# Reading Z and Bs back in the pieces that one unit wrote

## The chip, the cores and the metric

The kernel runs on one core of a Trainium2 chip. The metric is the device time of one execution in microseconds (us). The engines are PE (TensorE, matmuls), PEld (its weight loads), DVE (VectorE), ACT (ScalarE), POOL (GpSimd) and SP (SyncE, which here only issues DMAs). DMAs that SP issues stand in the profile's queue q1, those of POOL in q0; 16 DMA engines move the data of both.

## The reference

The kernel computes a Fourier layer with a feed-forward block behind it, for 8 sequences of 3008 rows of 256 values:

```
X = rfft(x, axis=1)                                # x: (8, 3008, 256)
Yr = Xr @ w_r - Xi @ w_i + b_r
Yi = Xr @ w_i + Xi @ w_r + b_i
Yr, Yi = soft-threshold of each at 0.01            # sign(Y) * max(|Y| - 0.01, 0)
y = irfft(Yr + i Yi, n=3008)
h = y @ w_in                                       # 256 -> 2048
out = elu(h) @ w_out                               # 2048 -> 256, float32
```

## The kernel before

3008 is 47 x 64, and both transforms are done as two matmul stages with a transposition between them. One sequence is a batch b, and its spectral part is cut into units, each a few matmuls into PSUM and one evacuation to bf16:

- A (`unit_A`, L129): 6 units, 4 of 24 column groups j each. M1 (128 x 128) makes the 64-point transform. The result, 128 rows (4 blocks of 32: half, real or imaginary) for each j, is written to a DRAM tensor DA [24, 128, 256].
- The transposition: `load_Z` (L159) reads DA back so that the 96 partitions of Z are (j, block) and the 32 slots of a block lie along the partition: row p = 4j + block. It is cut by slots, so that each read takes from all that the six A units wrote. Batch 0 has four reads of 8 slots (384 KB each), the others one of 8 and one of 24 slots.
- X (`unit_X`, L166): 8 units, two for every 8 slots. Each matmul contracts over the 96 partitions of one slot of Z with a table M2, whose rows are in the same order as those of Z.
- M (`m_group` L185, `unit_M`, `first_M` L220): 12 units, product with w_r and w_i, bias, soft-threshold. In steady batches the bias is the float tensor bias_bc, added on DVE (L202). In batch 0 some units have it added by PE instead (L189): a matmul of ones with bias_p, which holds the bias as three bf16 pieces in three of its rows.
- B (`unit_B`, L233): 6 units with table M3, written to DRAM as DB [24, 128, 256]. `load_Bs` (L267) reads it back as Bs, cut by slots like Z: four reads of 8 slots, 384 KB each, into four buffers.
- Y (`unit_Y`, L274): 8 units with table M4, two for each Bs read. They make yT, the input of the feed-forward part.

The feed-forward part runs over blocks of 512 rows: `front` (L705) multiplies with w_in and takes exponentials, `finish_elu` and `elu` finish the activation, `back` (L757) multiplies with w_out and stores. A batch has 47 steps of it. `plan` (L800) puts the spectral units of the next batches (b+1: X, M, B, Y; b+2: A) into the steps of batch b, one or two per step; `f0` runs ahead of a step's `front`, `f1` behind it. The order on each engine is the order of the program.

Batch 0's spectral part has nothing to run beside; this opening is written out by hand (L505 to L679), and its order matters here:

1. POOL reads x of batch 0 in six pieces between the iotas that make the tables. DVE and ACT make M1, then the A units run as x lands, each followed by its write of DA on SP.
2. Meanwhile DVE and ACT make M2 (`points`, `phases`, `wraps`, `sizes`, `signs`, `sines`), whose phases start from columns that depend on the row p (half and block: `qcol`, `c0`, `c1`).
3. SP then reads w_r and w_i (L518), Z in four pieces (L164), bias_bc (L527), and the first quarter of w_in (L578), which must wait until the scratch pool of the tables is free. POOL casts w_r and w_i to bf16 (L520 to L523).
4. On POOL a `gate` (a tiny copy that reads a landed tile, L588) holds back the reads of x for batch 1 until the second Z read has landed; behind them follows the first half of w_out (L583).
5. X units; between them DVE makes the three bias pieces (L602 to L610). Then M3 (L613 to L621), M and B units, DB writes, quarters 1 and 2 of w_in, and after the last B the Bs reads (L271), the A units of batch 1, the scaling of w_in (L658), and the first two Y units.

`idle_pe` (L295) issues matmuls without use that keep PE going.

Of the kernel before, what the change touches and what calls it, by code (L numbers as in the profile page):

```python
# [29 lines left out]
def kernel(  # L30
# [47 lines left out]
    zp = ctx.enter_context(tc.tile_pool(name="zp", bufs=1))  # L78
    wk2 = ctx.enter_context(tc.tile_pool(name="wk2", bufs=2))
    wk3 = ctx.enter_context(tc.tile_pool(name="wk3", bufs=3))  # L80
    wk4 = ctx.enter_context(tc.tile_pool(name="wk4", bufs=4))
# [47 lines left out]
    def unit_A(b, u, alone=False, on_dve=False, ahead=False):  # L129
        ci, uu = u // 2, u % 2  # L130
        if uu == 0:
            if ahead and ci > 0:
                A_of[b, ci] = late3.tile([P, 8, D], BF16, name="A", tag="gT")
            elif alone:
                A_of[b, ci] = wk4.tile([P, 8, D], BF16, name="A", tag="Bs")
            else:
                A_of[b, ci] = wk2.tile([P, 8, D], BF16, name="A", tag="A")
            if ci == 0:
                DA_of[b] = dram.tile([NJ, P, D], BF16, name="DA", tag="DA")
        xt, A = xts[ci], A_of[b, ci]  # L140
        dav = DA_of[b].rearrange("j p d -> p j d")
# [9 lines left out]
        )  # L151
        j0 = 8 * ci
# [6 lines left out]
    def load_Z(b, s0, s1):  # L159

        if b not in Z_of:
            Z_of[b] = zp.tile([2 * NR, NS, D], BF16, name="Z", tag="Z")
        dv = DA_of[b].rearrange("j (h c s) d -> (j h c) s d", h=2, c=2)
        nc.sync.dma_start(Z_of[b][:, s0:s1, :], dv[:, s0:s1, :])  # L164
# [102 lines left out]
    def load_Bs(b, w):  # L267

        Bs = wk4.tile([4 * K1, 8, D], BF16, name="Bs", tag="Bs")
        dv = DB_of[b].rearrange("k (c h m) d -> (k c h) m d", c=2, h=2)  # L270
        nc.sync.dma_start(Bs[:], dv[:, 8 * w : 8 * w + 8, :])  # L271
        Bs_of[b, w] = Bs

    def unit_Y(b, u, alone=False, on_dve=False):  # L274
# [3 lines left out]
        yT, Bs = yT_of[b], Bs_of[b, w]  # L278
        ps = unit_ps("yps", alone)
        psv = ps[:].rearrange("p a (k j) -> p (a k) j", j=P)  # L280
        for j in range(8):
            nc.tensor.matmul(  # L282
                psv[:, j, 0 : 2 * N1], lhsT=Bs[:, j, dt * P : dt * P + P], rhs=M4[:],
# [16 lines left out]
    brow, rest = (wk3.tile([P, 2 * D], F32, name="yb", tag="yb") for _ in range(2))  # L300
    nc.vector.memset(brow[:], 0.0)
    for o, bv in ((0, b_r), (D, b_i)):
        for k in range(3):
            nc.sync.dma_start(
                brow[32 * k : 32 * k + 1, o : o + D],
                bass.AP(tensor=bv.tensor, offset=bv.offset, ap=[[0, 1], [1, D]]),
            )
    idle_pe(9)
    xts = []
# [3 lines left out]
    with tc.tile_pool(name="stagep", bufs=1) as stagep:  # L313
# [41 lines left out]
        pcol = iota("pcol", [P, 1], [[0, 1]], cm=1)  # L355
        srow = iota("srow", [P, 2 * NS], [[0, 2], [1, NS]])
# [52 lines left out]

        k4h = col(dve, qcol, 0.5, ALU.mult, -0.25, ALU.add)  # L410
# [87 lines left out]
        pool.tensor_tensor(v4[:], v4[:], r4[:], ALU.subtract)  # L498

# [17 lines left out]
        fA(5)  # L517
        nc.sync.dma_start(w_r_f[:], w_r.rearrange("(c p) e -> p c e", p=P))  # L518
        nc.sync.dma_start(w_i_f[:], w_i.rearrange("(c p) e -> p c e", p=P))
        pool.tensor_copy(wcat_r[:, :, 0:D], w_r_f[:])  # L520
        pool.tensor_copy(wcat_r[:, :, D : 2 * D], w_i_f[:])
        pool.tensor_scalar(wcat_s[:, :, 0:D], w_i_f[:], -1.0, None, ALU.mult)
        pool.tensor_copy(wcat_s[:, :, D : 2 * D], w_r_f[:])  # L523
        for g in range(4):
            load_Z(0, 8 * g, 8 * g + 8)
# [36 lines left out]
        idle_pe(40)  # L562
# [10 lines left out]
    def load_w_in(q):  # L573
        if q < 3:
# [10 lines left out]
    def gate(src):  # L585

        t = gatep.tile([P, 1], F32, name="gate", tag="gate")
        nc.gpsimd.tensor_copy(t[0 : src.shape[0], :], src)  # L588
# [6 lines left out]
    gate(Z_of[0][:, 8, 0:1])  # L595
    for ci in range(3):
        load_x(1, ci)
    load_w_out(0)
    nc.vector.tensor_scalar(w3[:], v3[:], CMAGIC, -CMAGIC, ALU.add, ALU.add)
    nc.vector.tensor_tensor(w3[:], v3[:], w3[:], ALU.subtract)  # L600
    nc.scalar.copy(bias_p[:], brow[:])
    nc.vector.tensor_tensor(rest[:], brow[:], bias_p[:], ALU.subtract)  # L602
    for u in range(8):
        unit_X(0, u, alone=True, on_dve=u in (1, 4, 7))
        if u == 1:
            nc.scalar.activation(a3[:], w3[:], AF.Abs)
            nc.vector.tensor_copy(bias_p[32:64], rest[32:64])
            nc.vector.tensor_copy(bias_p[64:P], rest[64:P])
            nc.vector.tensor_tensor(rest[64:P], rest[64:P], bias_p[64:P], ALU.subtract)
            nc.vector.tensor_copy(bias_p[64:P], rest[64:P])  # L610
        idle_pe(1)
# [14 lines left out]
    nc.scalar.activation(r4[:], v4[:], AF.Sin, bias=0.0, scale=TURN)  # L626
    nc.scalar.activation(dume[:], busy[:, 0:1], AF.Exp, scale=0.0)
# [3 lines left out]
    load_w_in(1)  # L631
    first_M(2, 1, True)
    first_M(3, 0, False)
    fB(1)
    first_M(3, 1, True)
    first_M(4, 0, False)
    fB(2)
    first_M(4, 1, True)
    first_M(5, 0, True)
    fB(3)  # L640
    load_w_in(2)
    first_M(5, 1, True)
    let_go()
    fB(4)
    idle_pe(3)
    fB(5, True)
    M4v = M4[:].rearrange("p (a h) -> p a h", h=2)
# [4 lines left out]
    load_Bs(0, 0)  # L652
    load_Bs(0, 1)
# [8 lines left out]
    scale_w_in(0, True)  # L662
    for u in range(6):
        unit_A(1, u, on_dve=bool(u % 2), ahead=True)
        if u == 1:
            scale_w_in(1, True)
            for w in (2, 3):
                load_Bs(0, w)
            gate(Bs_of[0, 2][:, 0, 0:1])
            load_w_out(1)  # L670
            load_w_in(3)
        idle_pe(2)
    scale_w_in(2, False)
    for s0, s1 in ((0, 8), (8, NS)):
        load_Z(1, s0, s1)
# [124 lines left out]
    def plan(b):  # L800
# [18 lines left out]
        for t, u in enumerate(seq, lead):  # L819
# [9 lines left out]
            if u == ("A", 1):  # L829
# [69 lines left out]
```

## Time and profile before

| | us |
|---|---|
| time, median of 3 runs (912.48 to 912.52) | 912.52 |
| the profiled execution's own time | 911.36 |
| its span, first to last instruction | 909.6 |
| first A matmul | 5.93 |
| first read of Z issued | 18.40 |
| first X matmul | 23.25 |
| first M matmul | 29.77 |
| last B's matmuls end | 46.82 |
| first Y matmul | 55.16 |
| first `front` matmul | 56.54 |
| first Y of batch 1 | 149.35 |
| mean granted clock of TensorE | 0.997 |

Busy shares are taken over the whole span, so they hide the opening, a sixteenth of it. To read the opening one goes by the chain in order of time, which follows the work that ended last back through what released it, and by the timeline and the windows of the first 60 us.

### The profile page before, as it was taken

How to read it: one execution, taken by the hardware profiler on the slowest of the kernel's cores; microseconds unless marked ns; L12 is line 12 of the kernel's file. 1: busy time of each engine (PE TensorE's matmuls, PEld its weight loads, DVE VectorE, ACT ScalarE, POOL GpSimd, SP SyncE). 2: the span in 40 equal slices, each digit the busy share in tenths (PEclk: the TensorE clock that was granted, in tenths of full speed). 3: DMA queues.
4: the chain of work that ended last, by engine and by line, in shares of the span. 5: the costliest groups of instructions: out<-in, count | busy, mean ns of one | idle time of the engine just before them, and what ended most of it. 6: DMA issues, size and time to landing. Idle time of an engine off the chain costs nothing.

```text
span 909.6 us, 17270 instructions
## 1 busy us (share of the span) xinstructions
PE 893.2 (98%) x6721; PEld 652.3 (72%) x6721; DVE 717.5 (79%) x891; ACT 696.8 (77%) x850; POOL 314.9 (35%) x438
## 2 busy tenths in 40 slices
PE   8989999999999999999999999999999999999997
PEld 3447667876688667886678766787667866777775
DVE  8669778887788778897788877888778877778776
ACT  6768788777878778787787888778887877767664
POOL 6701540333321441405404153033332134443664
PEclk9999999999999999999999999999999999999999
DMA  8997116721283215732166032752228111231011
GB/s 270 309 269 228 47 48 186 209 70 47 77 241 124 71 47 143 190 109 85 56 201 194 24 99 59 217 161 72 69 72 230 30 42 47 82 82 48 24 48 46
DMA packets 90670, 106.24 MB, mean 117 GB/s; under 512 B 5270, under 2 KB 81308, under 8 KB 87228
## 3 DMA queue, kind: packets, MB, share of 16 engines
q1 hardware_dynamic: 84332, 77.62, 30.6%
q0 software_dynamic: 5968, 27.26, 9.1%
q8 instruction: 52, 0.85, 0.4%
q10 hardware_dynamic: 288, 0.26, 0.1%
q14 instruction: 30, 0.25, 0.1%
HBM read 55.32 MB, written 49.81 MB: 116 GB/s over the span
## 4 chain that ended last, share of the span: by engine, by line
PE 85%; DVE 5%; ACT 3%; DMA 3%; issue 2%; POOL 1%; SPq 1%; DVEq 0%; ACTq 0%; POOLq 0%
PE ps_o L773 34%; PE hps L715 34%; PE mps L192 9%; PE yps L282 2%; PE bps L244 2%; PE xps L175 2%; PE aps L144 2%; DMA Bs<-DB 2%; DVE gT L742 1%; DVE Et L754 1%; ACT Et L729 1%; ACT Et L726 1%; DMA xt<-in_x_dram 1%; DVE osb L784 1%; ACT Bz L257 1%
## 5 line engine op out<-in xcount | busy, mean ns | idle before, releaser
L773 PE MATMUL ps_o<-w_out_r,gT 128*128 128x256 f32 x3008 | 477.0, 301 | 0.2 <-DVE gT L740 0.2
L773 PEld LDWEIGHTS ps_o<-w_out_r,gT 128*128 128x128 f32 x3008 | 403.4, 189 | 50.3 <-DVE osb L784 1.3
L715 PE MATMUL hps<-yT,w_in_s 128*128 128x512 bf16 (+4 forms) x1728 | 389.9, 353 | 2.5 <-DVE gT L742 1.2
L740 DVE SCALAR_TENSOR_TENSOR gT<-Et,hps 128x512 fp32r<-128x512 f32 (+1 forms) x272 | 222.8, 848 | 75.3 <-POOL Et L752 38.2
L742 DVE SCALAR_TENSOR_TENSOR gT<-hps,Et 128x1024 fp32r<-128x1024 f32 x198 | 242.2, 1223 | 16.5 <-PE ps_o L773 1.0
L715 PEld LDWEIGHTS <-w_in_s 128*128 128x128 bf16 x1728 | 141.6, 98 | 129.4 <-issue 23.0
L729 ACT ACTIVATE Et<-hps 128x1024 f32<-128x1024 f32 x198 | 204.0, 1030 | 13.2 <-PE hps L715 6.7
L752 POOL TENSOR_SCALAR Et<-Et 128x512 f32<-128x512 f32 x187 | 111.4, 615 | 222.9 <-ACT Et L724 222.9
L754 DVE TENSOR_SCALAR Et<-Et 128x1024 f32<-128x1024 f32 x198 | 137.0, 692 | 48.0 <-ACT Et L729 40.1
L210 POOL TENSOR_SCALAR clip<-yb 128x512 f32<-128x512 f32 x84 | 51.7, 615 | 316.0 <-DVE yb L202 278.6
L724 ACT ACTIVATE Et<-hps 128x512 f32<-128x512 f32 x188 | 102.1, 595 | 63.9 <-PE hps L715 63.9
L726 ACT ACTIVATE Et<-hps 128x1024 f32<-128x1024 f32 x84 | 86.3, 1027 | 71.5 <-PE hps L715 71.0
L211 POOL TENSOR_TENSOR Y<-yb,clip 128x512 bf16<-128x512 f32 x84 | 107.2, 1276 | 7.0
L727 ACT ACTIVATE Et<-Et 128x1024 f32<-128x1024 f32 x84 | 88.8, 1058 | 2.7
L202 DVE TENSOR_TENSOR yb<-mps,bias_bc 128x512 f32<-128x512 f32 x89 | 61.4, 689 | 35.4 <-PE mps L192 28.6
L127 ACT CAST XT<-xps 128x768 bf16<-128x768 f32 x61 | 48.8, 800 | 15.8 <-PE xps L175 15.8
L127 ACT CAST yT<-yps 128x752 bf16<-128x752 f32 x63 | 49.7, 788 | 14.2 <-PE yps L282 14.1
L192 PE MATMUL mps<-wcat_r,XT 128*128 128x512 bf16 x192 | 58.2, 384 | 0.8 <-ACT Bz L257 0.3
L127 ACT CAST A<-aps 128x1024 bf16<-128x1024 f32 x45 | 45.6, 1014 | 15.3 <-PE aps L144 13.8
L192 PE MATMUL mps<-wcat_s,XT 128*128 128x512 bf16 x192 | 57.1, 379 | 0.0
L192 PEld LDWEIGHTS <-XT 128*128 128x128 bf16 x384 | 30.8, 98 | 29.6 <-DVE XT L125 0.6
L257 ACT CAST Bz<-bps 128x1024 bf16<-128x1024 f32 x46 | 46.0, 1000 | 2.5 <-PE bps L244 2.5
(110 smaller groups left out, 412.9 us busy)
## 6 DMA issues: line engine op xcount, KB each, us to landing
xt<-in_x_dram POOLq DMA_DIRECT2D x21, 1024.0 KB, 7.1
out_dram<-osb SPq DMA_DIRECT2D x158, 128.0 KB
Bs<-DB SPq DMA_DIRECT2D x32, 384.0 KB
DA<-A SPq DMA_DIRECT2D x21, 512.0 KB
DB<-Bz SPq DMA_DIRECT2D x21, 512.0 KB
Z<-DA SPq DMA_DIRECT2D x7, 1152.0 KB
Z<-DA SPq DMA_DIRECT2D x11, 384.0 KB
xt<-in_x_dram POOLq DMA_DIRECT2D x6, 512.0 KB, 5.9
```

Of the source, the lines that this page charges most:

```text
L127: nc.scalar.copy(dst, src)
L192: nc.tensor.matmul(ps, lhsT=XT[:, dt, c, o : o + P], rhs=wm[:, dt, :], start=(not biased and m == 0 and dt == 0), stop=(m == 1 and dt == 1),)
L211: nc.gpsimd.tensor_tensor(Y_of[b, q][:, i, :], yb, clip[:], ALU.subtract)
L715: nc.tensor.matmul(hps[:, s, c0:c1], lhsT=w_in_s[:, dt, ft * P : ft * P + P], rhs=yT_of[b][:, dt, t0 : t0 + c1 - c0], start=(dt == 0), sto ...
L724: nc.scalar.activation(E_[:, s], hps[:, s], AF.Exp)
L726: nc.scalar.activation(E_, hps[:], AF.Relu, scale=-1.0)
L729: nc.scalar.activation(E_, hps[:], AF.Exp)
L740: nc.vector.scalar_tensor_tensor(o, e, -1.0, h, ALU.add, ALU.max)
L742: nc.vector.scalar_tensor_tensor(o, h, 0.0, e, ALU.max, ALU.add)
L752: eng.tensor_scalar(E_[:, s], E_[:, s], 1.0, 0.0, ALU.min, ALU.max)
L754: nc.vector.tensor_scalar(E_, E_, 1.0, -1.0, ALU.min, ALU.add)
L773: nc.tensor.matmul(po[q][:, i_ % 2, :], lhsT=gT[:, s, i_ * P : i_ * P + P], rhs=w_out_r[:, ft, :], start=(ft == 0 and i_ % 2 == 0), stop=( ...
```

## The change

- **Reads of Z and Bs.** A read now takes what one unit wrote: the four j (or k) of unit u, 256 KB that lie together in DRAM, as 16 rows of 16 KB. They go to every sixth partition of Z, u, u + 6, ..., u + 90. There are six reads per batch for Z and six for Bs. Bs becomes one tile of all 32 slots in a pool with one buffer (batch 0's A shares it).
- **Tables.** The row p of Z and Bs now stands for i + 16u, where p = 6i + u. Seven more operations on DVE (`sixth` to `c0`) and one iota on POOL (`p16`) make this number as `zcol` and from it `qcol`, `c0`, `c1`, from which M2 and M4 follow as before.
- **Bias pieces.** The bias is read as 128 partitions of four values, split into three pieces by five small POOL operations, written to DRAM (`bd`) and read back into three rows of bias_p. The 128 x 512 arithmetic on DVE and ACT goes.
- **Opening requests.** SP: after the A writes come `bd`, Z reads 0 to 3, bias_p, Z reads 4 and 5, then w_r, w_i and bias_bc. The casts of w_r and w_i move from POOL to DVE, between X units. The wrap of M3's phase (`w3`) moves from DVE to POOL. The gate of batch 1's x now looks at w_i. Each Bs read of batch 0 follows one write of DB later on; w_in's quarter 1 stands behind the second of them, quarter 2 behind all six, quarter 3 behind A of batch 1. The absolute value for M3 moves behind the X units, the sine for M4 ahead of them, and the load of the Exp table behind the last B.
- **Steady batches.** Two Z reads follow each second A unit a step later, two Bs reads each second B unit (not ahead of the last Y unit of the batch before). w_in's quarters 2 and 3 are scaled by DVE in halves behind steps 1 to 4.

The diff, cut to its core:

```diff
-    def load_Z(b, s0, s1):
+    def load_Z(b, u):
 
         if b not in Z_of:
             Z_of[b] = zp.tile([2 * NR, NS, D], BF16, name="Z", tag="Z")
-        dv = DA_of[b].rearrange("j (h c s) d -> (j h c) s d", h=2, c=2)
-        nc.sync.dma_start(Z_of[b][:, s0:s1, :], dv[:, s0:s1, :])
+        dv = DA_of[b][4 * u : 4 * u + 4].rearrange("j (r s) d -> (j r) s d", r=4)
+        nc.sync.dma_start(Z_of[b][u : 2 * NR : 6], dv)
...
-    def load_Bs(b, w):
+    def load_Bs(b, v):
 
-        Bs = wk4.tile([4 * K1, 8, D], BF16, name="Bs", tag="Bs")
-        dv = DB_of[b].rearrange("k (c h m) d -> (k c h) m d", c=2, h=2)
-        nc.sync.dma_start(Bs[:], dv[:, 8 * w : 8 * w + 8, :])
-        Bs_of[b, w] = Bs
+        if b not in Bs_of:
+            Bs_of[b] = bsp.tile([P, NS, D], BF16, name="Bs", tag="Bs")
+        dv = DB_of[b][4 * v : 4 * v + 4].rearrange("k (r m) d -> (k r) m d", r=4)
+        nc.sync.dma_start(Bs_of[b][v : 4 * K1 : 6], dv)
...
-    brow, rest = (wk3.tile([P, 2 * D], F32, name="yb", tag="yb") for _ in range(2))
-    nc.vector.memset(brow[:], 0.0)
...
+    for o, bv in ((0, b_r), (P // 2, b_i)):
+        nc.sync.dma_start(b4[o : o + P // 2, :], bv.rearrange("(p j) -> p j", j=4))
+    bd = dram.tile([P, 3, 4], BF16, name="bd", tag="bd")
+    nc.vector.memset(bias_p[:], 0.0)
...
         pcol = iota("pcol", [P, 1], [[0, 1]], cm=1)
+        p16 = iota("p16", [P, 1], [[0, 1]], cm=16)
...
+        sixth = col(dve, pcol, 1.0 / 6.0, ALU.mult, -5.0 / 12.0, ALU.add)
+        rcol = col(dve, sixth, CMAGIC, ALU.add, -CMAGIC, ALU.add)
+        zcol = mix(dve, rcol, -95.0, p16, ALU.mult, ALU.add)
+        half = col(dve, zcol, 0.5, ALU.mult, -0.25, ALU.add)
+        qcol = col(dve, half, CMAGIC, ALU.add, -CMAGIC, ALU.add)
+        c1 = mix(dve, qcol, -2.0, zcol, ALU.mult, ALU.add)
+        c0 = col(dve, c1, -1.0, ALU.mult, 1.0, ALU.add)
...
+        for k in range(3):
+            pool.tensor_copy(bp3[:, k, :], b4[:])
+            if k < 2:
+                pool.tensor_tensor(b4[:], b4[:], bp3[:, k, :], ALU.subtract)
...
         fA(5)
+        nc.sync.dma_start(bd[:], bp3[:])
+        for u in range(6):
+            load_Z(0, u)
+            if u == 3:
+                nc.sync.dma_start(
+                    bias_p[0:3, :].rearrange("k (p j) -> k p j", j=4),
+                    bd.rearrange("p k j -> k p j"),
+                )
         nc.sync.dma_start(w_r_f[:], w_r.rearrange("(c p) e -> p c e", p=P))
         nc.sync.dma_start(w_i_f[:], w_i.rearrange("(c p) e -> p c e", p=P))
-        pool.tensor_copy(wcat_r[:, :, 0:D], w_r_f[:])
...
-        for g in range(4):
-            load_Z(0, 8 * g, 8 * g + 8)
...
+        nc.scalar.activation(r4[:], v4[:], AF.Sin, bias=0.0, scale=TURN)
+        pool.tensor_scalar(w3[:], v3[:], CMAGIC, -CMAGIC, ALU.add, ALU.add)
+        pool.tensor_tensor(w3[:], v3[:], w3[:], ALU.subtract)
+        idle_pe(37)
...
+        for u in range(8):
+            unit_X(0, u, alone=True, on_dve=u in (1, 4, 7))
+            if u in (1, 4):
+                for dst, src, sc in casts[u // 2 : u // 2 + 2]:
+                    dve.tensor_scalar(dst, src[:], sc, None, ALU.mult)
+            if u == 0:
+                t = stagep.tile([P, 1], F32, name="gate")
+                pool.tensor_copy(t[:], w_i_f[:, 1, D - 1 : D])
+                for ci in range(3):
+                    load_x(1, ci)
+            idle_pe(1)
...
     load_w_in(0)
-    gate(Z_of[0][:, 8, 0:1])
-    for ci in range(3):
-        load_x(1, ci)
     load_w_out(0)
...
+    nc.scalar.activation(a3[:], w3[:], AF.Abs)
...
     fB(1)
+    load_Bs(0, 0)
...
     fB(2)
+    load_Bs(0, 1)
+    load_w_in(1)
...
     fB(3)
-    load_w_in(2)
+    load_Bs(0, 2)
...
     fB(4)
+    load_Bs(0, 3)
     idle_pe(3)
     fB(5, True)
+    load_Bs(0, 4)
+    load_Bs(0, 5)
+    load_w_in(2)
+    nc.scalar.activation(dume[:], busy[:, 0:1], AF.Exp, scale=0.0)
...
     scale_w_in(0, True)
+    gate(Bs_of[0], 64, 4 * K1, 0)
+    load_w_out(1)
     for u in range(6):
         unit_A(1, u, on_dve=bool(u % 2), ahead=True)
+        if u % 2:
+            write_A(1, u)
...
-            if u == ("A", 1):
-                f1[t] += [(load_Bs, (n1, w)) for w in range(4)]
-            if u == ("A", 5) and n2 < B:
-                f1[t] += [(load_Z, (n2, s0, s1)) for s0, s1 in ((0, 8), (8, NS))]
+            if u[0] == "B" and u[1] % 2:
+                at_ = max(t, seq.index(("y", 7)) + lead) + 1
+                f1[at_] += [(load_Bs, (n1, u[1] - 1)), (load_Bs, (n1, u[1]))]
+            if u[0] == "A" and u[1] % 2 and n2 < B:
+                f1[t + (u[1] < 5)] += [(load_Z, (n2, u[1] - 1)), (load_Z, (n2, u[1]))]
```

## The prediction

> **What bounds the kernel now.** I read the page first, then the chain of work in order of time, then the opening's timeline, windows and DMA answers. The page says that this is a TensorE kernel:
>
> ```profile
> span 909.6 us, 17270 instructions
> PE 893.2 (98%) x6721; PEld 652.3 (72%) x6721; DVE 717.5 (79%) x891; ACT 696.8 (77%) x850; POOL 314.9 (35%) x438
> ```
>
> After about 57 us the chain is nearly all matmuls, and a read that is early there is worth nothing. The chain in order of time shows where transfers set the end (start, length, what):
>
> ```profile
> 6.12 7.21 DMA xt<-in_x_dram
> ...
> 29.48 0.97 DVE XT L125
> ...
> 30.50 0.82 PE mps L192 x3
> ...
> 48.19 2.77 DMA DB<-A
> ...
> 51.15 3.97 DMA Bs<-DB
> ...
> 55.16 0.85 PE yps L282 x16
> ```
>
> The reader is to see one round trip of DB on the path: write 2.77, read 3.97. The round trip of DA is not in the chain but in the timeline:
>
> ```profile
> 18.40 1.74 SPq L164 DMA_DIRECT2D Z<-DA  x4
> ...
> 23.25 0.51 PE L175 MATMUL xps<-M,Z 96*128 96x96 bf16 x8 [0.43 <-DMA Z<-DA]
> ```
>
> The four reads of Z are issued from 18.40, when all of DA is written, and the first X starts at 23.25 with only the first of them landed; the seventh X waited for the fourth read, until 27.63. In the steady part PE's waits show Bs late twice, at 149.35 and 797.83:
>
> ```profile
> PE yps L282 <- DMA Bs<-DB: 1.9, 2, 1.0
> ```
>
> The DMA engines themselves are full for most of the opening (columns end with clock, DMA share, GB/s), and while POOL's queue has a transfer going, a younger one of SP's does not move: DB's first write is issued at 36.82, and the DMA answer for 37 to 39 us lists it among the issues but has packets of q0 (POOL's) alone:
>
> ```profile
> 36.00:38.00 2.00, 2.00 (x15) 0.85 (x15) 0.64 (x2) 0.80 (x1) 1.83 (x3) 1.00 1.22 379
> ...
> q0 software_dynamic: 685, 0.75, 161.6%
> ...
> DB<-Bz SPq DMA_DIRECT2D x1, 256.0 KB
> ```
>
> The packet records say the same for DA's first write (issued 7.85, first packet about 11.4, when the reads of x end).
>
> **The change, step by step**, for batch 0 (times before -> after).
>
> *Ahead of Z.* One more iota stands ahead of the reads of x on POOL: 0.14 (row of pcol): all reads of x, and DA's last write, +0.14. Seven one-column operations on DVE (0.15 to 0.17 each, 1.1 in all) delay the tables; DVE idles 0.73 at 12.73 and the tables end near 21.5, ahead of the first X: nothing, as long as X does not start before 21.6. The three bias pieces are five small POOL operations (0.19 to 0.58) after 13.84: done by 14.9 to 16.9, beside DA's last packets, which end at 17.3: nothing.
>
> *Z.* SP has the six reads behind DA's writes; the first four need only writes that landed long before, so their packets follow DA's at 17.3 where they began at 19.2 (w_r and w_i, 0.5 MB, went first): -1.9. Against it, every X contracts over all 96 partitions, so the first X now needs all six reads, not one of four. The same 1.5 MB goes to the same rows, now as 16 rows of 16 KB a read, one for each of 16 DMA engines. By the packet records a 4 KB packet took 0.245 us, a 12 KB one of Z 0.80: 16 KB is 1.0 to 1.07, six of them 6.0 to 6.4, as 24 of 4 KB were (5.9). I take the old landing of the last read: 27.63 - 1.9 + 0.14 = 25.9. The read of bias_p stands ahead of the last two reads: 384 packets of 8 bytes. The nearest rows are 9 ns (4 bytes) and 27 ns (512 bytes): spread over 16 engines 0.2 to 0.65, on fewer engines more (rival 4); I take 0.3. First X: 23.25 -> 26.2, **+2.95**.
>
> *X.* Eight units; ACT has five evacuations of 0.80, DVE three of 0.95, and PSUM two buffers. The 3.15 us of bias arithmetic leave DVE, four casts of weights (0.42, row of w_in_s 128x512) come in, each pair right after an evacuation and done before DVE's next one. Stepping the two buffers through gives 6.5 from first X to last evacuation; before it was 7.2. First M: 30.50 -> 32.7, **+2.2**. The casts need w_i at 28.3: its packets end about 26.8 (25.3 + 32 packets of 46 ns an engine); just covered.
>
> *M and B.* The absolute value for M3 (0.85) stood between X units on ACT; now it and two sines (0.85, 0.92) follow the last X, and DVE's product for M3 (0.96) stands ahead of the first M's bias add on DVE, which comes 1.1 later after the first M. Three PSUM buffers absorb part: PE loses between 0 and 0.9, I take 0.6. PE is full from there (2.00 of 2.00 in the windows). Last B ends 46.83 -> 49.6, **+2.8**. The wrap of M3's phase on POOL (0.92 + 1.91 from its 128x512 rows) ends near 24.7: hidden. The Exp table load (1.28 + 0.20) moves behind the last B, ahead of the first A of batch 1 on ACT.
>
> *Bs.* The reads of x for batch 1 now wait for w_i (27.6, gate 0.4, issue 28.1, was 26.19): with w_out's first half they hold the engines until 41.4 (was 39.5). SP's first quarter of w_in waits for the casts (about 31 instead of 25.6): it is younger than these, so it goes after 41.4, and so do DB's writes. Behind 41.4 stand two quarters of w_in (1.3 each), six writes (0.8), six reads of Bs (1.0), and SP waits in order: each read for its write's landing (packets' end + 0.9), with the next write queued behind it. Stepped through, DB's last write lands at 54.8 (was 50.97) and the last read at 57.7: 54.9 + 0.9 to the first packet + 1.0 + 0.9. Y could not start before 57.5 anyway (last B + 7.9: table load, six units of A in two PSUM buffers, then a buffer). First Y: 55.15 -> 57.8, **+2.65**.
>
> *Later.* Batch 1's Z: last read lands about 74 and X comes at 75.4: nothing, at most 2. From batch 1 on, four of six Bs reads and of six Z reads come long before need: a gain off the path. The two places where Bs is late now need the last two reads (512 KB, 2.0) instead of the first of four (384 KB, six packets of 0.245: 1.5): +0.5 each, **+1.0**; if something else than the size held them, these waits could vanish (-2.2). w_in's scaling in DVE's halves (0.42) is covered in slots that PE bounds.
>
> Sum: 2.65 + 1.0 = **+3.65 us**. Against the profiled execution (span 909.6, time 911.36) that is 915.0; the median of the runs, 912.52, lies 1.16 above it, so I predict 916.2.
>
> **Rivals.**
> 1. *Read rate* (faster). Reads with one 16 KB run an engine could go at the rate of x's rows (8 KB in 0.325): 0.65 instead of 1.0 each. Then all of Z lands at 17.3 + 3.9 + 0.9 + 0.44 = 22.5, the first M comes 1.5 earlier, and the first Y is set by A at 45.9 + 7.9 = 53.8: -1.35; late waits -0.3; without the 0.6 in M -2.25: 910.3 to 910.9, say 910.5. It decides where a Z packet of 16 KB takes under about 0.8. For it: the first Z packets of 4 KB took 0.18. Against: 12 KB packets took 0.80, and instruction fetches of 16 KB 1.05.
> 2. *It washes out.* If Z's stragglers come from the bias reads mixed in behind them (last packet near 26.8, the mass done by 25.3), Z lands at 24, the first M and the last B stay where they are, Y starts with A's end at 54.7 to 55.3, and the late waits add up to 1.0: +0 to +1.1, say 913.1.
> The Trainium skill (SBUF — State Buffer, Door 1: The DMA port swizzle) puts 64 of these 96 partitions on one half of the ports. Its 435 GB/s over 16 ports would make their 1 MB over eight ports an estimate of 4.8 us, where the packet rows make 6.0 for Z; by the page Z would land at 23.4, the first Y come at 54.7, and the time be about 912.3.
> 3. *The reads go one by one.* It doesn't do what it says, if every sixth partition counts as an overlap with the read before: each read then waits for the last one's landing, 3.5 apiece (3.97 less 0.5). Z would land near 36, the first Y near 68, +13, and late Bs +1 to 3: 927.
> 4. *bias_p's packets on few engines* (slower). If its 384 small packets go to as many engines as it has rows, three, each of these has 128 of them ahead of the last two reads of Z: at 9 to 27 ns 1.2 to 3.5 us instead of the 0.3 in the sum, so the first X and all behind it 0.9 to 3.2 later: 918.2. For it: only stragglers decide when Z has landed. Against: those engines may be early otherwise.
> The Trainium skill (DMA: Bandwidth & Descriptors, Why a DMA increments its semaphore by 16 and not by 1) has this rule: a DMA runs on the largest number of engines, up to 16, that divides the slowest dimension of both sides, which here is three. No row of this trace shows such a transfer.
>
> **Chances.** Forecast 0.45, read rate 0.15, washes out 0.17, one by one 0.10, bias_p 0.13. A measurement of this kernel tells about 0.2% (1.8 us) from no change. Faster 0.15 (read rate), same 0.17 (washes out), slower 0.68 (the other three). The range goes from 909 (read rate, and the late waits gone) to 922 (bias_p at 3.5, M at 0.9, batch 1's Z 2 late); one by one is left out.
>
> **What would show it.** The first Z packets right behind DA's last at 17.3; the first X near 26 released by Z, and X's eight units in 6.5; no pause of SP between reads of Z beyond DA's; no packet of w_in or DB between 30 and 41; the first Y released by Bs near 57.8; the two late waits at about 1.4 each. I am wrong if the first X comes before 24.5, if w_in's first quarter flows beside the reads of x, or if the steady part changes by more than 2 us.

## The result, and the profile after

| | before | after | ratio, 95% interval |
|---|---|---|---|
| median on record, us | 912.52 | 928.32 | 1.0164 [1.0149, 1.0179] |
| the same kernel once more (e1), us | 912.37 | 926.43 | 1.0148 [1.0129, 1.0167] |

Slower by 14 to 16 us, where +3.65 was forecast, and above the range. Five of the six executions on record lie between 926.7 and 929.1; the profiled one took 3,089 us, with its matmuls two to three times as long throughout, and nothing is read from it: the profile after is that of e1 (time 927.73).

> The changed kernel as it is, for a profile at full matmul speed (the profiled execution on record ran its matmuls at about a third of their speed for its whole length, so it tells nothing of the waits). Measured so far: 926.7 to 929.1 us, 14 to 16 over the kernel before. The theory of the prediction's sum (all six reads of Z before the first X, then a DMA backlog in front of Bs) expects the first X at 26.2, the first M at 32.7 and the first Y at 57.8, and can explain 4 us of the 15; the rest would have to show as a later first Y or as a slower steady part. Rival 'the reads go one by one' expects pauses of about 3 us of SP between the Z reads, Z landed near 36 and the first Y near 68. Rival 'bias_p's packets on few engines' expects the first X 1 to 3 us after 26.2, released by Z. A further rival, that the loss is in the steady part, expects the first Y below 60 and over 10 us lost after it.

The page of after, span and busy time:

```profile
span 925.9 us, 17323 instructions
PE 900.3 (97%) x6718; PEld 658.4 (71%) x6718; DVE 714.6 (77%) x897; ACT 696.2 (75%) x848; POOL 315.1 (34%) x442
```

PE is busy 7 us longer, for three matmuls fewer. SP's queue and PE in after's timeline, the place of the four reads of Z and the first X:

```profile
16.67 2.49 SPq L171 DMA_DIRECT2D Z<-DA  x4
19.44 0.32 SPq L540 DMA_DIRECT2D bias_p<-bd  x1
19.81 4.66 SPq L171 DMA_DIRECT2D Z<-DA  x2
24.51 0.59 SPq L544 DMA_DIRECT2D w_r_f<-in_w_r_dram  x1
...
28.77 0.80 PE L182 MATMUL xps<-M,Z 96*128 96x96 bf16 x8 [6.27 <-DMA Z<-DA]
```

The first X stands at 28.77 instead of 23.25, and PE waited 6.27 for it. The sign that SP makes no pause between the reads of Z failed: behind bias_p's read it is held for 4.02 us in the issue of the fifth. The windows of after (columns end with the granted clock of TensorE as a share of its full clock, the DMA share, and GB/s):

```profile
26.00:28.00 2.00, 0.00 (x0) 0.00 (x0) 0.00 (x0) 0.00 (x0) 0.61 (x1) 0.50 0.69 160
28.00:30.00 2.00, 1.24 (x12) 0.99 (x13) 0.00 (x0) 0.40 (x1) 0.19 (x1) 0.50 0.87 265
30.00:32.00 2.00, 2.00 (x19) 1.45 (x18) 1.33 (x3) 0.67 (x2) 1.75 (x3) 0.50 0.43 59
```

Two things are to be seen: the granted clock is at half while X runs (1.00 from 24 to 30 in before), and at 30 to 32 the DMA engines move 59 GB/s (393 in before, 420 in e2): w_i has landed, and the reads of x, which wait for it, are issued at 30.25. The chain in order of time goes on:

```profile
23.88 4.54 DMA Z<-DA
...
43.18 1.73 PE mps L199 x8
...
61.43 1.09 PE ips L306 x5
62.52 1.16 issue
63.68 0.51 PE yps L289 x8
...
65.62 11.77 DMA w_in_f<-in_moe_w_in_dram
```

The round trip of DB is no longer in it; in its place stand A of batch 1 and, after the first Y, the last quarter of w_in, 11.77 us from issue to landing. From 85 us on, PE's waits have the two late Bs still, not longer but shorter:

```profile
PE yps L289 <- DMA Bs<-DB: 1.6, 2, 1.2
```

Where the loss stands is read from milestones. ps_o's matmuls, those with w_out, come in 374 groups, nearly all of eight; "ninth group" is when the ninth starts, and "steady" the stretch from there to the start of the 361st. Each row is one profiled execution; ratios are of all runs to those of before on the same chip.

| kernel | time, ratio | first X | last B ends | first Y | ninth group | steady |
|---|---|---|---|---|---|---|
| before | 912.52 | 23.25 | 46.82 | 55.16 | 80.24 | 797.15 |
| e2 before again | 912.68 | 24.02 | 48.32 | 56.48 | 81.70 | 796.98 |
| e1 after | 1.0148 | 28.77 | 53.93 | 63.68 | 91.45 | 801.31 |
| e3 bias_p last | 1.0145 [1.0128, 1.0162] | 28.33 | 53.46 | 63.29 | 90.09 | 801.06 |
| e4 PE kept busy | 1.0177 [1.0160, 1.0193] | 28.64 | 51.79 | 64.78 | 93.39 | 801.18 |
| e5 w_in earlier | 1.0164 [1.0148, 1.0179] | 29.08 | 53.97 | 64.01 | 92.99 | 801.22 |
| e6 gT moved | 1.0115 [1.0098, 1.0132] | 28.59 | 53.65 | 63.10 | 90.34 | 797.99 |
| e8 pieces alone | 1.0292 [1.0277, 1.0307] | 28.33 | 53.04 | 64.76 | 90.31 | 814.27 |
| e10 w_out late | 1.0190 [1.0175, 1.0205] | 28.34 | 52.80 | 61.56 | 92.23 | 801.11 |
| e11 gate on Z | 1.0146 [1.0119, 1.0173] | 28.17 | 52.37 | 61.68 | 91.59 | 800.95 |
| e12 writes first | 1.0134 [1.0109, 1.0160] | 28.31 | 53.25 | 61.69 | 88.40 | 801.05 |
| e13 together | 1.0076 [1.0052, 1.0100] | 27.66 | 50.83 | 59.25 | 87.58 | 797.94 |
| e14 before, one read | 1.0051 [1.0034, 1.0069] | 28.09 | 52.95 | 60.94 | 86.05 | 796.37 |
| e15 before, shifted | 1.0048 [1.0031, 1.0065] | 22.79 | 47.45 | 55.83 | 81.24 | 801.01 |

Two executions of one kernel differ in the opening: before and e2 by 0.8 at the first X and 1.3 at the first Y, and where the requests up to X are after's (e1, e4, e5, e6, e10, e11, e12), the first X lies between 28.17 and 29.08. Smaller differences between two rows are not told apart from that.

After (e1) against e2, by spans 15.05 us: the first Y 7.20 late, 2.55 more by the ninth group, 4.33 in the steady stretch, 0.97 behind it. My theory after this reading: Z is late because bias_p's small packets hold SP (19.81 to 23.83), the half clock stretches X, w_in's last quarter comes late, and gT's new place slows ps_o. Rivals: the six pieces themselves cost it, or the transfers are late as a whole, and each repair only moves a wait.

### The profile page after: what moved, and what is told of

The parts are those of the page before. It is cut to its first block, busy times and chain, and to the rows that moved or that the text cites. A ratio compares the mean times of both kernels' runs of the same rounds, so it can differ in the third digit from the quotient of the medians.

```text
span 3087.6 us, 17323 instructions
## 1 busy us (share of the span) xinstructions
PE 3081.0 (100%) x6718; PEld 1861.9 (60%) x6718; DVE 722.5 (23%) x897; ACT 716.4 (23%) x848; POOL 312.9 (10%) x442
## 4 chain that ended last, share of the span: by engine, by line
PE 100%; DVE 0%; issue 0%
PE hps L740 39%; PE ps_o L798 38%; PE mps L199 10%; PE xps L182 3%; PE bps L251 2%; PE aps L145 2%; PE yps L289 2%; PE ips L306 2%; PE mps L196 0%; DVE yT L125 0%; DVE osb L809 0%; DVE busy L300 0%
## 5 line engine op out<-in xcount | busy, mean ns | idle before, releaser
L798 PE MATMUL ps_o<-w_out_r,gT 128*128 128x256 f32 x3008 | 1516.1, 734 | 0.0
L798 PEld LDWEIGHTS ps_o<-w_out_r,gT 128*128 128x128 f32 x3008 | 1241.9, 463 | 325.9 <-issue 306.7
L740 PE MATMUL hps<-yT,w_in_s 128*128 128x512 bf16 (+4 forms) x1728 | 1285.0, 963 | 0.2 <-DVE yT L125 0.2
L740 PEld LDWEIGHTS <-w_in_s 128*128 128x128 bf16 x1728 | 322.0, 210 | 599.8 <-issue 593.4
L209 DVE TENSOR_TENSOR yb<-mps,bias_bc 128x512 f32<-128x512 f32 x89 | 61.5, 691 | 567.6 <-PE mps L199 511.3
L199 PE MATMUL mps<-wcat_s,XT 128*128 128x512 bf16 x192 | 188.2, 1130 | 0.0
L199 PE MATMUL mps<-wcat_r,XT 128*128 128x512 bf16 x192 | 185.6, 1099 | 0.0
L199 PEld LDWEIGHTS <-XT 128*128 128x128 bf16 x384 | 75.4, 231 | 140.5 <-issue 139.4
L145 PE MATMUL aps<-xt,M 128*128 128x512 f32 x96 | 97.2, 1125 | 0.0
L182 PE MATMUL xps<-M,Z 96*128 96x96 bf16 x512 | 95.6, 423 | 0.0
L289 PE MATMUL yps<-M,Bs 96*128 96x94 bf16 x512 | 90.6, 407 | 0.0
```

What stands on the lines that cost most here:

```text
L145: nc.tensor.matmul(ps[:, j, :], lhsT=M1[:], rhs=xt[:, 4 * uu + 2 * j : 4 * uu + 2 * j + 2, :], start=True, stop=True,)
L182: nc.tensor.matmul(psv[:, kk, 0 : 4 * K1], lhsT=Z[:, k, dt * P : dt * P + P], rhs=M2[:, k].rearrange("p c m -> p (c m)"), start=True, stop ...
L199: nc.tensor.matmul(ps, lhsT=XT[:, dt, c, o : o + P], rhs=wm[:, dt, :], start=(not biased and m == 0 and dt == 0), stop=(m == 1 and dt == 1),)
L289: nc.tensor.matmul(psv[:, j, 0 : 2 * N1], lhsT=Bs[0 : 4 * K1, 8 * w + j, dt * P : dt * P + P], rhs=M4[:], start=True, stop=True,)
L740: nc.tensor.matmul(hps[:, s, c0:c1], lhsT=w_in_s[:, dt, ft * P : ft * P + P], rhs=yT_of[b][:, dt, t0 : t0 + c1 - c0], start=(dt == 0), sto ...
L798: nc.tensor.matmul(po[q][:, i_ % 2, :], lhsT=gT[:, s, i_ * P : i_ * P + P], rhs=w_out_r[:, ft, :], start=(ft == 0 and i_ % 2 == 0), stop=( ...
```

## The experiments

### The steady part: where gT lies

The pitch is the mean time from the start of one ps_o matmul to that of the next in its group; by that measure it is 141.7 ns in before and 143.8 in after (e1). e2 is before, unchanged, profiled on another chip.

> The kernel before, profiled once more on the chip that runs the next kernels. The float32 matmuls that write ps_o have a mean pitch of 141.5 ns in the trace of before and 143.6 in the trace of after, 3,000 of them, and after's shift grows from 11.2 to 15.5 us over the steady part. Theory 1 (the kernel does it, by where its tiles lie): 141.5 here. Rival (the two traces come from two chips): up to 143.6 here, and a span some 4 us over the 909.6 of the first trace.

Its ps_o pitch is 141.7 ns: the 2 ns are the kernel's. In the compiled kernels gT's buffers begin 64 bytes later in after (the new tiles b4 and bp3 stand ahead of them); the traces hold no addresses, so what the runs can show is what a pad of 64 bytes does. e15 shifts before, e6 shifts after by 64 bytes more:

```diff
+    constp.tile([P, 16], F32, name="pad")
```

> Before, with a tile of 64 bytes more in the constants, so that gT and what lies behind it stand 64 bytes off a multiple of 128 as in after; no instruction changes. Theory 1 (the place of gT makes the ps_o matmuls slower): their mean pitch 143.5 ns instead of 141.6, the steady part (ninth to 361st group) 801 us instead of 797.1, the opening unchanged, time 3.5 to 5 us above before's. Rival (it takes the pieces' reads beside them): pitch 141.6, time within 0.7 of before's.

> After, with a tile of 64 bytes more in the constants, so that gT lies at a multiple of 128 bytes again as in before (in after it lies 64 bytes off); nothing else changes. Theory 1 (the slower float32 matmuls of ps_o, mean pitch 143.6 ns against 141.6 in the two traces of before, come from where gT lies): the pitch is back at 141.6, the steady part (ninth to 361st group of ps_o matmuls) takes 797.0 to 797.4 us instead of 801.3, and the time is 3.5 to 5 us below after's. Rival (they come from the reads of Z and Bs that run beside them): pitch 143.6 and time within 1 us of after's.

The groups of ps_o on the pages of before, e15, after and e6 (us in total, mean ns of one):

```profile
L773 PE MATMUL ps_o<-w_out_r,gT 128*128 128x256 f32 x3008 | 477.0, 301 | 0.2 <-DVE gT L740 0.2
```

```profile
L774 PE MATMUL ps_o<-w_out_r,gT 128*128 128x256 f32 x3008 | 483.3, 303 | 0.2 <-DVE gT L741 0.2
```

```profile
L798 PE MATMUL ps_o<-w_out_r,gT 128*128 128x256 f32 x3008 | 483.2, 303 | 0.2 <-DVE gT L765 0.2
```

```profile
L799 PE MATMUL ps_o<-w_out_r,gT 128*128 128x256 f32 x3008 | 478.7, 301 | 0.2 <-DVE gT L766 0.2
```

Before with nothing but the shift is 4.3 us slower (916.82 against 912.56, pitch 143.8); after with gT back on a multiple of 128 gets most of its steady stretch back (797.99, pitch 142.3; 797.15 and 141.7 in before) and is 3.3 us below e1 (923.11 against 926.43). Settled: 3.3 to 4.3 us of the loss are an address. That gT is the tile is argued: of the two tiles that these matmuls read, w_out_r is made ahead of the pad in the kernel's text and gT behind it, and the pitch of the other kinds of matmul is unchanged. gT was not moved alone. It is the operand that is loaded as weights (`lhsT`); one load takes 188 to 189 ns in the mean in all four kernels, and the matmuls behind it stand farther apart.

### The first X

e3 moves bias_p's read behind all others:

```diff
             load_Z(0, u)
-            if u == 3:
-                nc.sync.dma_start(bias_p[0:3, :]..., bd...)
...
+        nc.sync.dma_start(bias_p[0:3, :]..., bd...)     # behind bias_bc
```

> After, with the read of bias_p behind all reads of Z, w_r, w_i and bias_bc. Theory 1 (its 384 small packets keep SP in the issue of the fifth Z read from 19.8 to 23.8): the six Z reads are issued back to back, the sixth near 20.9, Z is landed at 25.9 to 26.6, the first X comes at 26.3 to 27.0 instead of 28.8, PE's half clock behind it gets shorter, and the time is 2 to 4 us below after's. Rival (six reads of 16 KB rows are slow by themselves, bias_p only stands beside them): the first X stays within 0.5 of 28.8 and the time within 1 us of after's.

SP issued all six reads by 20.26, and the first X moved by 0.44 only, which is inside the spread named above: my theory fell. That SP was held for 4 us cost little; Z's last packet ended 0.7 earlier without it (26.83 for 27.57). e14 leaves before as it is, with one read in place of four:

```diff
-        for g in range(4):
-            load_Z(0, 8 * g, 8 * g + 8)
+        load_Z(0, 0, NS)
```

> Before, with one read of all of Z in batch 0 in place of four, in the same place among the requests: rows of 16 KB to all 96 partitions, no pieces by unit, and the first X waits for all of it. Theory 1 (waiting for all of Z costs the first X what it loses, with pieces or without): first X at 27.5 to 28.5 as with the six pieces (28.33 in the kernel with the pieces alone), first M at 34.5 to 36, first Y 2 to 4 later than before's 55.2 to 56.5, time 914 to 917. Rival (the pieces are slow for where their rows go): first X at 26.5 or earlier.

```profile
28.09 0.82 PE L175 MATMUL xps<-M,Z 96*128 96x96 bf16 x8 [5.19 <-DMA Z<-DA]
```

The first X comes at 28.09, without any piece, and the time is +4.4. So waiting for all of Z is the cost of X, as the prediction had it, and no more is seen for the pieces' layout. e8 is before with the pieces and tables, and before's order of requests:

```diff
-        for g in range(4):
-            load_Z(0, 8 * g, 8 * g + 8)
+        for u in range(6):
+            load_Z(0, u)
...
+    for v in range(6):
+        load_Bs(0, v)                               # behind the last B
...
+                f1[t] += [(load_Bs, (n1, v)) for v in range(6)]
```

> Before, with the six reads of Z and Bs and the tables in that order alone: the requests of the opening stay in before's order, w_r and w_i ahead of Z, six reads in place of four, all six of Bs behind the last B. gT lies where it lies in before. Theory 1 (the other order of the requests and the place of gT make the loss, the pieces only what their wait for all six reads costs): first X at 27.6 to 29 with a half clock behind it, first Y at 57 to 60, ps_o pitch 141.6, steady part as before's 797, time 915 to 919. Rival (the pieces make the loss): first Y at 62 or later, or a steady part of 800 or more, and a time of 922 or more.

First X at 28.33 again, with w_r and w_i ahead of Z. The rival is right about the rest: 938.6, because Y now needs all six reads, and they were issued at the old times. PE's waits of e8, over the whole kernel (4.4 of the 15.7 stand ahead of the first Y):

```profile
PE yps L284 <- DMA Bs<-DB: 15.7, 5, 4.8
```

In after the same pieces are issued earlier, behind each pair of units, and that is worth some 16 us of the steady stretch (814.27 in e8; 797.99 in e6, where gT lies as in before).

### The first Y

e4 has idle_pe(62) for idle_pe(37) ahead of X.

> After, with 62 instead of 37 matmuls without use ahead of the first X, so that PE has work until about 28. Theory 1 (PE's 6.3 us without work bring the half clock from 24.7 to 35.0): the granted clock stays at 1.0 there, the X stage takes 6.5 to 7.0 instead of 8.5 us, and the time is 1 to 2.5 us below after's. Rival (X is bound by ACT's and DVE's evacuations and casts): the clock is full, and the X stage still takes 8 us or more; time within 0.7 us of after's.

From e4's windows and its timeline, POOL and PE:

```profile
28.00:30.00 2.00, 1.28 (x18) 0.91 (x19) 0.26 (x1) 0.80 (x1) 0.00 (x0) 1.00 0.77 225
30.00:32.00 2.00, 1.97 (x27) 1.31 (x27) 1.50 (x4) 1.44 (x2) 0.63 (x2) 1.00 0.23 60
...
31.81 2.00 POOL L116 DMA_DIRECT2D xt<-in_x_dram  x3
...
64.78 1.41 PE L289 MATMUL yps<-M,Bs 96*128 96x94 bf16 x16 [4.42 <-DMA Bs<-DB]
```

The clock stayed full, X took 6.4 us to its last evacuation instead of 8.5, the first M and the last B came 2.1 us earlier, and the first Y 1.1 later: PE then waited 4.42 for Bs. Why the gate saw w_i 1.6 later in this run is open; but it shows the second limit. In e1, e3, e4, e5 and e11 the first Y stands 32.8 to 33.5 behind the issue of x for batch 1, while it stands 9.3 to 13.0 behind the last B. The other limit is batch 1's A: in e12 and e13, where Y waits for no transfer, it comes 8.4 behind the last B (the prediction took 7.9). In after they lie at 62.4 (53.93 + 8.4) and 63.7. e10, e11 and e12 each pull at the transfers:

```diff
-    load_w_out(0)                                   # e10: to behind the gate on Bs
...
-                pool.tensor_copy(t[:], w_i_f[:, 1, D - 1 : D])
+                pool.tensor_copy(t[64:96, :], Z_of[0][64:96, 0, 0:1])    # e11
...
     fB(4)
-    load_Bs(0, 3)                                   # e12
     fB(5, True)
+    load_Bs(0, 3)
```

> After, with the first half of w_out read behind the gate on Bs, right ahead of the second half, instead of behind the reads of x for batch 1. Theory 1 (the first Y is set by the backlog of requests that x and w_out put ahead of DB's writes, which move only when w_out has landed at 45.1): DB's first write lands some 3 us earlier, its last read with it, and the first Y comes at 60 to 61.5 instead of 63.7; then the first ps_o matmuls wait for w_out, so that the time is between 2 us below after's and 3 above. Rival (the first Y is set by the last B and the round trip of its write): first Y within 0.7 of 63.7.

> After, with the gate that holds back the reads of x for batch 1 looking at Z instead of w_i, so that they are issued at about 28.9 instead of 30.25 and follow w_i's packets without the pause of 1.4 us that after has at 30 to 31.5. Theory 1 (the first Y is set by the backlog of requests, which begins with these reads): w_out lands 1.3 earlier, the first Y comes 1.0 to 1.5 earlier, at 62.2 to 62.7, and the time is 1 to 1.5 below after's. Rival (the first Y is set by the last B and the round trip of DB): first X and last B as in after, first Y within 0.5 of 63.7, time within 0.7.

> After, with the fourth read of Bs issued behind the last write of DB, so that this write no longer stands in SP's queue behind a read that waits for an earlier write's landing. Theory 1 (SP's order holds the last write from about 55 to 56.94, and its round trip sets the first Y): the last write is issued at about 55, the first Y comes 1.5 to 2 us earlier, and the time is 1 to 2 us below after's. Rival (the transfers themselves are the limit, from whichever queue): first Y within 0.6 of 63.7, time within 0.7.

All three bring the first Y forward by 2.0 to 2.1, to within 0.9 of A's limit. In e10 the first Y (61.56) is just outside the 60 to 61.5 expected, 1.1 of the gain is the last B's, and w_out is then missing; the bracket of PE's line has the idle time ahead of the first ps_o:

```profile
71.74 2.08 PE L798 MATMUL ps_o<-w_out_r,gT 128*128 128x256 f32 x8 [3.32 <-DMA w_out_r<-in_moe_w_out_dram]
```

In e11 the last B came 1.6 earlier too, so it does not tell the two limits apart, and its gain is gone by the ninth group (91.59 against 91.45). In e12 the last write of DB, the second of its pair, is issued at 54.62, 2.3 earlier than in after (0.7 of it because the last B is). SP's queue in e12 and in after:

```profile
53.00 1.98 SPq L267 DMA_DIRECT2D DB<-A  x2
```

```profile
56.94 0.53 SPq L267 DMA_DIRECT2D DB<-A  x1
```

Only e12 keeps its gain, 924.6 against 926.4 in e1, though the intervals of the two ratios overlap.

### The first steps

e5 reads w_in's last quarter between two writes of DA. e13 puts the repairs together; e16, e17 and e18 change e13's order of requests.

```diff
     for u in range(6):
         unit_A(1, u, on_dve=bool(u % 2), ahead=True)
         if u % 2:
             write_A(1, u)
+        if u == 1:
+            load_w_in(3)                            # e5
...
-    load_w_in(3)
```

> After, with the read of w_in's last quarter right behind the second write of DA instead of behind all three. Theory 1 (this quarter, issued at 65.6 and landed at 77.4, is waited for by its scaling on DVE, 1.8 us, and PE behind it): that wait is gone, the shift against before no longer grows from 8.8 to 11.2 in the first steps, and the time is 1.5 to 2.5 us below after's. Rival (PE is held there by the write of DA and by A itself): the scaling comes sooner and the time stays within 0.7 us of after's.

DVE in after and in e5:

```profile
77.42 0.43 DVE L684 TENSOR_SCALAR w_in_s<-w_in_f 128x512 bf16<-128x512 f32 x1 [1.81 <-DMA w_in_f<-in_moe_w_in_dram]
```

```profile
76.48 1.22 DVE L768 SCALAR_TENSOR_TENSOR gT<-hps,Et 128x1024 fp32r<-128x1024 f32 x1 [3.50 <-DMA DA<-A]
```

The wait for w_in went, and one for a write of DA, whose tile shares gT's buffers, took its place: no gain (927.26 against 926.43 in e1), as the rival had it in kind.

> After, with all of these: w_r and w_i ahead of Z as in before, bias_p behind all reads, the gate on Z, the last write of DB ahead of the fourth read of Bs, 54 matmuls without use ahead of X, and gT at a multiple of 128 bytes. Theory 1 (the opening's backlog and gT's place make the loss): first X at 28 to 28.6 with a full clock, x for batch 1 issued 1.5 us earlier, first Y at 59 to 60.5, steady part (ninth to 361st ps_o group) 797.5 to 798, time 916 to 919. Rival (what the pieces themselves cost stays): first Y at 62 or later and time of 921 or more.

e13 (w_r and w_i ahead of Z, bias_p last, idle_pe(54), and the edits of e6, e11 and e12) takes 919.57, between the two forecasts. The opening is ahead of after by 4.4 at the first Y, the steady stretch is within 1.0 of before's, but from the first group of ps_o to the ninth it takes 21.8 us where before takes 18.3.

```diff
# e16: on e13
+    load_w_in(3)                                    # right behind load_w_in(2)
...
-    gate(Bs_of[0], 64, 4 * K1, 0)
-    load_w_out(1)                                   # to behind the A units
# e17: on e16
-    gate(Bs_of[0], 64, 4 * K1, 0)
+    gate(A_of[1, 2], 64, 4 * K1, 7)
# e18: on e13
     fB(0)
+    load_w_in(1)
...
     fB(3)
+    load_w_in(2)
...
+    load_w_in(3)                                    # behind the last Bs read
```

> The version with all repairs (e13), with w_in's last quarter read right behind its third, ahead of the writes of DA, and the second half of w_out behind all A units. Theory 1 (the order of these requests holds the first steps: DVE waited 2.3 us for w_in's last quarter and 1.9 for a write of DA): both waits are gone, the first nine ps_o groups take 18.5 to 19.5 us instead of 21.8, and the time is 2 to 3.3 below e13's 919.6. Rival (the bytes themselves are late, and the wait moves to the next one in the queue, as it did when the last quarter was read between two writes of DA): 21 us or more, and a time within 1 us of e13's.

> The kernel of e16, with the gate of w_out's second half looking at batch 1's last A tile instead of Bs, so that this half is issued no earlier than the last write of DA. Theory 1 (the write of DA that gT waits for stands behind the 1 MB of w_out): DVE's wait of 4.8 us for DA falls below 2.5, the first nine ps_o groups take 19 to 21 us instead of 23.6, and the time is 2.5 to 5 below e16's 924.1. Rival (the write is late for itself: its packets, or SP's issue of it, which took 4.8 us): the wait stays above 4 and the time within 1.5 of e16's.

> The version with all repairs (e13), with w_in's quarters where before has them: quarter 1 behind the first B, quarter 2 behind the fourth, and quarter 3 ahead of batch 1's writes of DA. Theory 1 (the change moved two quarters, 1 MB, out of the M and B stage, in which the DMA engines are about half busy, to behind Bs, where they delay w_in's last quarter and the write of DA that DVE waits for): first nine ps_o groups in 18.3 to 19.5 us instead of 21.8, first Y within 0.7 of 59.25, time 2 to 3.5 below e13's 919.6. Rival (DB's writes and Bs's reads wait for the quarters put ahead of them, so that the first Y comes later by what the first steps gain): first Y at 60.3 or later, time within 1 of e13's.

| | time, ratio | first X | last B ends | first Y | ninth group |
|---|---|---|---|---|---|
| e13 | 919.57, 1.0076 [1.0052, 1.0100] | 27.66 | 50.83 | 59.25 | 87.58 |
| e16 | 924.12, 1.0124 [1.0101, 1.0146] | 27.45 | 50.62 | 59.05 | 89.23 |
| e17 | 925.07, 1.0126 [1.0101, 1.0150] | 28.51 | 52.73 | 61.14 | 92.17 |
| e18 | 919.77, 1.0093 [1.0065, 1.0121] | 28.46 | 52.67 | 62.01 | 87.28 |

The longest waits of DVE for a transfer there, in e13, e16 and e17 (us in total, times, longest); e18 has none over 1.0:

```profile
DVE w_in_s L684 <- DMA w_in_f<-in_moe_w_in_dram: 2.3, 1, 2.3
DVE gT L767 <- DMA DA<-A: 1.9, 1, 1.9
```

```profile
DVE gT L767 <- DMA DA<-A: 4.8, 1, 4.8
```

```profile
DVE gT L767 <- DMA DA<-A: 4.7, 1, 4.7
```

In e16 the wait moves to the next request, as the rival had it, and the median is 4.5 us above e13's; the profiled execution, the fastest of e16's, shows 1.5 of that.

In e17 the wait stays, the rival's sign: the write was issued first (61.54, w_out at 62.06) and still landed no sooner; SP needed 4.5 us to issue it, and from 66 to 67 the records hold 205 packets of w_out beside 271 of the write. The Trainium skill (DMA: Bandwidth & Descriptors, Queues, rings and completion order) says that an engine goes round between the queues that have work; this trace agrees. My reading of before, that a younger transfer of SP's stands still behind POOL's, was too strong: in after w_in's first quarter, issued at 35.63, has its first packet at 39.21, as the reads of x end (31.6 to 40.3), but then 113 packets from 40 to 41 beside 97 of w_out's, which was issued earlier (32.07).

e18 has before's first steps again (17.7 us from the first group to the ninth), starts them later, and ends where e13 does. Only 0.9 of the later start is the quarters': the first Y stands 9.3 behind the last B, in e13 8.4. The other 1.8 is the last B's, and it was there before the first request that e18 moves: X began 0.8 later and ran at half clock from 29.8 to 33.2, in e13 at full clock. e17 differs from e16 in the same way (half clock from 28.4 to 31.8). So these two rows compare less well than their edits suggest, and that the moved quarters alone made the slow first steps is not shown, since a later start also leaves the transfers more time. What sets the ninth group in e13 is not settled; in e18 its delay against e2, 5.6, is the first Y's, 5.5.

### PE's clock in before

e9 has idle_pe(8) for idle_pe(3) ahead of before's first Y.

> Before, with 8 instead of 3 matmuls without use ahead of its first Y, so that PE has work until Bs lands. Theory 1 (PE's idle time ahead of the first Y brings the half clock of 57.5 to 60.9 in before): the clock is full there and the time 0.5 to 1.7 us below before's. Rival (the half clock comes from something else, or the first steps are bound by other engines): within 0.3 us of before's, or slower by as much as the extra matmuls delay the first Y.

The half clock of 58 to 60 us is gone (granted 1.00 in every window), and the time is 912.37 against 912.15, 1.0002 [0.9993, 1.0011]: the rival's. From the first group of ps_o to the ninth it takes 19.7 instead of 18.3. No version that was tried beats before.

## Why the prediction was wrong, point by point

- **Ahead of Z**, tables and bias pieces: right; nothing of them is late.
- **Z** is the step that failed first. Waiting for all six reads was sized rightly: 23.25 to 27.63 on paper, 28.09 in e14. The credit of 1.9 for putting Z ahead of w_r and w_i does not exist. By the packet records of e1 Z's first 16 packets of 16 KB started at 18.1, not 17.3, and took 2.03 us each, and all 96 took 1.25 in the mean, not 1.0 to 1.07: six times 0.2 and the start 0.8 later make up 2.0. (17.3 was misread: in before DA's last packet ends at 17.77.) With w_r and w_i ahead again (e13, e16, e17, e18) X comes at 27.45 to 28.51, no later than with Z ahead (28.17 to 29.08), and the packets take 1.10 to 1.15. I had taken the durations from reads that stood behind other packets. That empty engines make the first packets slow is not shown: in e5, with after's requests, the first 16 took 1.30, and started 1.0 later.
- **X**: 8.5 instead of 6.5 from first X to last evacuation, because PE, without work for 6.3 us, ran at half clock. The evacuations were stepped through rightly (e4, at full clock: 6.4). What the half clock cost by itself is not told: in e4 the last B came 2.1 earlier, but the reads of x were issued 1.6 later, and they set the first Y there.
- **M and B**: +0.3 to +0.4 where +0.6 was taken; the last B is late because X is (53.93 for 49.6).
- **Bs**: the first Y was set by what the step named, with both limits right in kind. The terms were off: the reads of x were issued at 30.25 instead of 28.1, because w_i stands last in the line that the slower Z leads, and a pause of the DMA engines came with it; the fourth read of Bs held the last write of DB for about 1.6 us (e12), a wait that the step names and gives no price of its own. First Y +7.2 to +8.5 for +2.65.
- **Later** failed twice. The steady part was written off as unchanged by looking at requests alone; gT's place cost 4.3, over the 2 us that the prediction itself named as a sign of being wrong. And of w_in the step counts only the scaling, as covered; it has no term for two quarters that were moved behind reads of Bs: 2.55 between the first Y and the ninth group. With the old places that stretch is before's again (e18), but the steps also begin later there, so the cause is in part argued. The +1.0 for the late Bs has the wrong sign (1.6 for 1.9), since the pieces are issued earlier; e8 shows what they cost when they are not.
- **Rivals.** One by one gave 927, near the result, by a mechanism that is not there: four reads are issued within 2.49 us. Read rate and washing out: Z's packets took 9.5 us from first to last, not 4 to 6. bias_p on few engines: in e3, where they come last in SP's line, the first twelve of its 384 packets start 6 ns apart, and then 51 in every 100 ns, three times as many. The Trainium skill's rule (DMA: Bandwidth & Descriptors, Why a DMA increments its semaphore by 16 and not by 1) gives three engines here, and this trace agrees. They ran for 0.9 us there and 1.0 in e1, and cost at most 0.4 at X (e3) instead of 0.9 to 3.2.

The sum by measured terms, e1 against e2: first Y 7.2, first steps 2.55, steady 4.33, tail 0.97, for a forecast of 2.65, 0, 1.0 and 0. The way, slower, was right, and so were the waits named on the way to the first Y; the sizes were not, and half of the loss stands behind the first Y, where the sum has 1.0.

## What to carry to other kernels

A request that is moved to the head of a line gains only if its transfer runs there at the speed that it had in the line, and where the line as a whole is late, a wait that is taken away comes back at the next request: so look at its first late transfer, and not only at the wait that the chain shows. (No version here made Z early, so that this would repair the opening is not shown.) Before an edit with new tiles is judged, look where the hot matmul's operands have moved to; the test is a pad in the kernel before, which changes no instruction.

## What was not expected of the hardware

- float32 matmuls (128x128 by 128x256) whose weights, gT, lie 64 bytes off a multiple of 128 by the compiled kernels had a pitch of 143.8 instead of 141.7 ns, and the kernel was 0.48% slower (e15).
- With Z ahead of w_r and w_i the first 16 packets of 16 KB took 1.7 to 2.4 us in seven profiles of eight (1.3 in e5), later ones 1.1; with w_r and w_i ahead of Z the first took 1.0 to 1.3 (e13, e16, e17, e18).
- SP was held for 4.0 us in the issue of a read behind 384 packets of 8 bytes (e1), and for 4.5 and 4.8 in that of a third 512 KB write, while two writes and 1 MB of w_in ahead of it in its queue were still under way (e17, e16).
- The half clock comes in stretches of 3.4, 6.8 or 10.2 us in all these profiles (the one at a kernel's end aside). In e1 PE was busy for 1.20 of the 3.41 us ahead of such a stretch (24.7 to 35.0), its last matmul 2.2 us back; within it 2.77 busy of 3.42 did not bring the full clock back, and 3.41 of 3.41 did, 6.2 us after the first X.
